# One-token transformer block with cached attention: the values of six of eight steps loaded and multiplied four heads at a time

## The chip, the cores and the metric

The kernel runs on one core of a Trainium2 chip, in fp32 throughout. Five engines work side by side, each through its own list of instructions in order: PE (TensorE, matrix products; its weight loads are shown as PEld), DVE (VectorE), ACT (ScalarE), POOL (GpSimd) and SP (SyncE, which here only issues loads and stores). A wait on a semaphore holds up everything behind it on the same engine. Loads are carried by 16 DMA engines. The metric is device time in microseconds (us) of one execution, lower is better.

## What is computed

Batch 2, one new token, model width 512, 32 query heads that share 8 key/value heads (4 to 1), head width 128. Keys and values come from caches of 32768 positions, of which only the last W = 4096 are read. All weights and the cache window, 97.5 MB, are read once.

```python
mod = (silu(c) @ w_mod).reshape(2, 6, 1, 512)        # sa, ca, ga, sb, cb, gb
h = layernorm(x) * (1 + ca) + sa
q = (h @ wq)                                         # 2 x 32 heads x 128
p = softmax(q . k_cache[:, :, -4096:] * 128**-0.5)   # 4 query heads per key head
x = x + ga * ((p . v_cache[:, :, -4096:]) @ wo)
h = layernorm(x) * (1 + cb) + sb
x = x + gb * (silu(h @ w1) @ w2)
```

## The kernel before

**Loads.** All large loads go through one SBUF ring of 8 slots, 16 KB per partition each (`stream`, lines 70 to 75), in the order in which the program asks for them: `w_mod` (3 slots), `wq` (4 slots), then keys and values of the eight attention steps, then `wo`, `w1`, `w2` in pieces. SP issues all of them. A load into a slot waits until whatever read the slot's old contents is done: DVE for keys, PE for values and weights. The small inputs differ: `c` is loaded by four loads that ACT issues (line 109), `x` by one that SP issues between `w_mod` and `wq` (line 113). Both go into the tile `xc`, which DVE clears first (line 102). Every DMA signals one of eight semaphores, taken in turn over all issuing engines; the ninth DMA takes the first one again and is not issued before the earlier load on that semaphore has landed completely.

**Attention.** There are eight steps. Step s covers two key heads of one batch row (`divmod(s, B)`, line 80), with 4096 KB of keys and 4096 KB of values (`load_pair`, 32 KB per partition). `fetch(s + 1)` asks for the keys of step s + 1 and the values of step s. In a step:

- `keys(s, j)`, j = 0 to 3 (line 349): DVE transposes the keys in 32 x 32 blocks, eight instructions; four buffers hold the results.
- `scores(s, j)` (line 362): PE multiplies them with the queries, 16 products of 512 columns. In the trace every fp32 product is two records.
- `maxima` and `exponentials` (lines 372 to 394): the maxima per query head, a small product that turns them, the bias, the exponential on ACT.
- `turn` (lines 406 to 423): DVE transposes the probabilities (xp) and masks them (zp), PE spreads them with four products (pT), and two ACT copies write them into `ptb`, the weights for the values.
- `weighted` (line 436): 16 products of 512 columns against the values, and an ACT copy of the sum (ob, line 446); `collect` (line 454) adds it into `o_all`.

`turn`, `weighted` and `collect` of a step stand one step later on the engines, beside the key work of the next step. `inorder` keeps what it wraps in program order on its engine; the rest is placed by a scheduler. `place(1)` (lines 303 to 317) prepares the queries of the second half of the heads and stands in step 2.

**The tail.** `o_all` is divided by the row sums (on, line 526) and spread (oq, line 533) into `oTn` (line 536). Then `busy(6)` (line 559) issues six products whose result nothing reads; they keep PE running until `wo` is there. Then come the products with `wo` (acc_o, line 573), the second layer norm, `w1` (hid, line 621), silu, `w2` (acc_yw, acc_y, acc_l, lines 655 to 680) and the store (line 698).

Of the kernel before, what the change touches and what calls it, by code (L numbers as in the profile page):

```python
# [23 lines left out]
def adaln_block(  # L24
# [45 lines left out]
    def stream(n=1):  # L70
# [3 lines left out]
        turn_of[0] = i + n  # L74
        return slots[:, i % RING : i % RING + n, :].rearrange("p s e -> p (s e)")

    def load_pair(cache, s):


        i, b = divmod(s, B)  # L80
        t = stream(2)
        nc.sync.dma_start(
            t,
            cache[b, 2 * i : 2 * i + 2, SK - W :, :].rearrange("e (u n) d -> u e (n d)", u=P // 2),
        )
        return t

    def load_runs(w, per, lo, hi):
# [17 lines left out]
    rows8 = lambda t: t.rearrange("(ab r) m -> ab r m", r=16)[:, 0, :]  # L106
    for b in range(B):
        for lo in (0, 2):
            nc.scalar.dma_start(
                c_sp.rearrange("(g y) m -> g y m", g=4)[lo : lo + 2, 16 * b, :],  # L110
                c[b].rearrange("(g m) -> g m", m=P)[lo : lo + 2],
            )
    nc.sync.dma_start(rows8(x_sp), x2.rearrange("b (g m) -> g b m", m=P))
    wqt = load_runs(wq, 4, 0, 4)


# [31 lines left out]
        id16[:, :, None].to_broadcast([P, 16, 2]),  # L148
        half[:, None, :].to_broadcast([P, 16, 2]),
    )  # L150
    odd = const([P, 2], "odd")
    nc.vector.tensor_reduce(
        odd, ident.rearrange("p (a r) -> p r a", r=2), axis=AX.X, op=ALU.add
# [15 lines left out]
    nc.gpsimd.tensor_copy(  # L169
        selh[:, :, 2 * HQ - 8 : 2 * HQ].rearrange("p m (e g) -> p m e g", e=2),  # L170
        id4.rearrange("p (e m g) -> p m e g", e=2, g=G),
    )

    quad = const([P, 4, P], "quad")
# [20 lines left out]
    for t in mrow:  # L195
        nc.gpsimd.memset(t, 0.0)

    ptb = [const([P, 16, 2, 16], f"ptb{i}") for i in range(2)]
# [6 lines left out]
    oTn = const([P, 32, 32], "oTn")  # L205
    nc.gpsimd.memset(oTn, 0.0)
    mod_sp = const([P, 4, P], "mod_sp")
    x1 = const([P, P], "x1")

# [124 lines left out]
    kt, vt, wot, kT = {}, {}, [], {}  # L334
    s_ps, pr, o_ps, o_sb = {}, {}, {}, {}

    def fetch(s):

        if s < STEPS:
            kt[s] = load_pair(k_cache, s)  # L340
        if s > 0:
            vt[s - 1] = load_pair(v_cache, s - 1)

    def keys(s, j):


        kT[s, j] = ktp.tile([P, 64, 32], F32, tag="kT", name=f"kT{s}_{j}")
        for c in range(2):
            inorder(nc.vector.transpose(  # L349
                kT[s, j][:, 32 * c : 32 * c + 32, :],  # L350
                kt[s].rearrange("p (n j r) -> p j n r", j=4, r=32)[:, j, 32 * c : 32 * c + 32, :],
            ))

    def scores(s, j):

        if j == 0:
            s_ps[s] = bank("A", f"s{s}")
        i, b = divmod(s, B)
        for c in range(2):
            for e in range(2):  # L360
                r, h = 64 * e + 32 * c, 2 * i + e
                inorder(nc.tensor.matmul(  # L362
                    s_ps[s][r : r + 32, :],
                    qbd[h // 4][:, h % 4, b, j, :],
                    kT[s, j][:, 32 * c : 32 * c + 32, e:32:2],
                    start=(j == 0),
                    stop=(j == 3),
                ))
# [17 lines left out]
        ))  # L386

    def exponentials(s):
        bp = bank("B", f"bp{s}")
# [4 lines left out]
        inorder(nc.scalar.activation(  # L394
            pr[s].rearrange("p t k -> p (t k)"),
            s_ps[s],
            AF.Exp,
            bias=bias,
            scale=SCALE,
            accum_out=rowsum[:, s : s + 1],  # L400
        ))

    def turn(s):

        xp = once.tile([P, 16, 32], F32, tag="xp", name=f"xp{s}")
        inorder(nc.vector.transpose(xp, pr[s]))  # L406
        zp = once.tile([P, 4, 16, 16], F32, tag="zp", name=f"zp{s}")
        inorder(nc.vector.tensor_mul(  # L408
            zp,
            xp[:, None, :, 0:16].to_broadcast([P, 4, 16, 16]),  # L410
            quarter[:, :, None, None].to_broadcast([P, 4, 16, 16]),
        ))
        tp = bank("C", f"pT{s}")[:, : 2 * P]
        for i in range(4):
            inorder(nc.tensor.matmul(  # L415
                tp[32 * i : 32 * i + 32, :],
                mix.rearrange("p v e -> p (v e)"),
                zp.rearrange("p y t x -> p (y t) x")[:, :, 4 * i : 4 * i + 4],
                start=True,
                stop=True,  # L420
            ))
        for e in range(2):
            inorder(nc.scalar.activation(  # L423
                ptb[s % 2][:, :, e, :],
                tp.rearrange("p (w z) -> p w z", z=16),
                AF.Copy,
                scale=odd[:, e : e + 1],
            ))

    def weighted(s):  # L430
# [14 lines left out]
        o_sb[s] = once.tile([P, 4 * DH], F32, tag="wide", name=f"ob{s}")  # L445
        inorder(nc.scalar.copy(o_sb[s], o_ps[s]))  # L446

    def collect(s):

        i, b = divmod(s, B)  # L450
        lo = 2 * HQ - 8 - (HQ * b + 2 * G * i)
        for m in range(4):
            r = 64 * (m % 2)
            inorder(nc.tensor.matmul(  # L454
                o_all[r : r + 64, :],
                selh[:, m, lo : lo + 2 * HQ],
                o_sb[s][:, m * DH : (m + 1) * DH],
                start=(s == 0 and m < 2),
                stop=(s == STEPS - 1 and m >= 2),
                skip_group_check=True,  # L460
            ))

    fetch(0)
    keys(0, 0)
    for s in range(STEPS + 1):
        if s < STEPS:
            fetch(s + 1)
            scores(s, 0)
        if s > 0 and s != STEPS - 1:
            turn(s - 1)  # L470
        if s > 1:
            collect(s - 2)
        if s == 2:
            place(1)
        if s < STEPS:
            for j in range(1, 4):
                keys(s, j)
                scores(s, j)
            maxima(s)
            exponentials(s)  # L480
        if s < STEPS - 2:
            keys(s + 1, 0)
        if s > 0:
            weighted(s - 1)
        if s == STEPS - 2:
            turn(s)
            keys(s + 1, 0)
    collect(STEPS - 1)
# [67 lines left out]
    def busy(n):  # L556

        for _ in range(n):
            inorder(nc.tensor.matmul(  # L559
                junk[0:32, :],  # L560
                id4,
                quad.rearrange("p m y -> p (m y)"),
                start=True,
                stop=True,
            ))
# [1 line left out]

    acc = bank("D", "acc_o")
    ao = bank("A", "ao")[:, :P]
    busy(6)  # L570
    for q in range(28):
        g = q % 4
        inorder(nc.tensor.matmul(  # L573
# [152 lines left out]
```

## Time and profile before

| what | value |
|---|---|
| three runs | 235.96, 235.50, 235.21 us; median 235.5 |
| span of the profiled execution (first to last instruction) | 233.6 us |
| what the median has beyond that span | 1.9 us |
| busy PE / PEld / DVE / ACT / POOL | 160.1 / 42.0 / 114.8 / 28.9 / 10.5 us |
| loads and stores on SP's queue | 3768 packets, 97.53 MB, busy 97.2% of 16 engines' span |
| mean granted TensorE clock | 0.927 |

The span lacks what lies around the instructions; the profiled execution's own time is taken as its span plus the 1.9 us by which the median of the runs exceeds it. Rows of the timeline give start and length in us, the engine, the line of the kernel, the operation, out<-in and how many instructions were merged; the bracket behind a row says how long the engine had been idle before and what released it. In the chain of waits each piece starts where the one before released it.

### The profile page before, as it was taken

Reading aid. Unit: us, or ns where it says so; the run is one execution under the profiler, and the core shown is the slowest. Engines: PE = TensorE matmul, PEld = TensorE weight load, DVE = VectorE, ACT = ScalarE, POOL = GpSimd, SP = SyncE. Lnnn points to the kernel's source line nnn. Section 1 sums busy time; section 2 is a strip of 40 time slices with the busy share of each in tenths; the row PEclk is TensorE's granted clock in tenths of the full one; section 3 lists DMA queues with packets and bytes.
Section 4 is the critical chain, followed back from the end, with each engine's and each line's share of the span. In section 5 each row is a group of like instructions: output and inputs, shape, how many; then the busy total and the mean of one; then the engine's idle time right before and its main releaser. Section 6 shows DMA issues by size and latency. Waiting matters only on the chain.

```text
span 233.6 us, 2565 instructions
## 1 busy us (share of the span) xinstructions
PE 160.1 (69%) x1070; PEld 42.0 (18%) x1070; DVE 114.8 (49%) x171; ACT 28.9 (12%) x65; POOL 10.5 (5%) x35
## 2 busy tenths in 40 slices
PE   0004806949687839787679759759769778789784
PEld 0001301201111111211111201201111122324222
DVE  3004310278794758696197179249559540101232
ACT  1100300000311120120210201111030030102020
POOL 8600000000000000000000000000000000000000
PEclk9999965988799976999999979997999997999999
DMA  7998998999999999999999999999999999989991
GB/s 269 438 551 359 393 505 359 440 449 415 415 432 449 436 438 415 421 438 446 443 426 415 424 443 449 438 421 421 424 450 438 443 407 463 463 351 439 425 409 66
DMA packets 3794, 97.68 MB, mean 418 GB/s; under 512 B 432, under 2 KB 456, under 8 KB 968
## 3 DMA queue, kind: packets, MB, share of 16 engines
q1 hardware_dynamic: 3768, 97.53, 97.2%
q8 instruction: 8, 0.13, 0.2%
q14 instruction: 2, 0.02, 0.0%
q10 hardware_dynamic: 16, 0.00, 0.0%
HBM read 97.53 MB, written 0.00 MB: 418 GB/s over the span
## 4 chain that ended last, share of the span: by engine, by line
DMA 60%; issue 18%; DVE 14%; PE 6%; POOL 1%; SPq 0%; POOLq 0%; ACT 0%; DVEq 0%
DMA slots<-in_A_k_cache_dram 22%; DMA slots<-in_A_wq_dram 14%; DMA slots<-in_A_v_cache_dram 12%; DMA slots<-in_B_w_dram 12%; DVE kT L349 11%; PE o L436 2%; PE q L290 2%; DVE zp L408 1%; PE acc_yw L655 1%; DVE xp L406 1%; PE acc_y L665 0%; DVE xc L102 0%; DVE qT L303 0%; POOL qg L307 0%; PE acc_y L546 0%
## 5 line engine op out<-in xcount | busy, mean ns | idle before, releaser
L349 DVE STREAM_TRANSPOSE kT<-slots 128x1024 f32<-128x1024 f32 x64 | 73.7, 1210 | 23.6 <-DMA slots<-in_A_k_cache_dram 23.6
L362 PE MATMUL s<-kT,qbd 128*32 128x512 f32 x256 | 70.5, 703 | 18.9 <-DVE kT L349 17.9
L436 PE MATMUL o<-slots,ptb 128*32 128x512 f32 x256 | 30.8, 624 | 2.1 <-DMA slots<-in_A_v_cache_dram 2.1
L362 PEld LDWEIGHTS s<-kT,qbd 128*32 128x32 f32 x256 | 9.9, 114 | 69.5 <-DVE kT L349 65.1
L259 PE MATMUL m_a<-slots,scT 128*32 128x256 f32 x32 | 2.9, 446 | 20.5 <-DVE scT L251 20.5
L290 PE MATMUL q<-slots,hq_T 128*32 128x512 f32 x64 | 8.7, 707 | 9.0 <-DMA slots<-in_A_wq_dram 9.0
L436 PEld LDWEIGHTS o<-slots,ptb 128*32 128x32 f32 x256 | 8.1, 113 | 17.9 <-issue 17.8
L392 ACT COPY bias<-bp 128x1 f32<-128x1 f32 x8 | 1.3, 159 | 77.1 <-PE bp L390 77.1
L372 DVE TENSOR_REDUCE mx<-s 128x1 f32<-128x512 f32 x8 | 5.5, 692 | 9.5 <-PE s L362 9.5
L559 PE MATMUL junk<-quad,id 128*32 128x512 f32 x22 | 10.2, 595 | 0.0
L408 DVE TENSOR_TENSOR zp<-xp,quarter 128x1024 f32<-128x1024 f32 x8 | 9.8, 1225 | 0.2
L423 ACT ACTIVATE ptb<-pT,odd 128x256 f32<-128x256 f32 x16 | 6.7, 473 | 25.7 <-PE pT L415 25.7
L303 DVE STREAM_TRANSPOSE qT<-q 128x512 f32<-128x512 f32 x2 | 1.4, 718 | 14.2 <-PE q L290 12.7
L446 ACT COPY ob<-o 128x512 f32<-128x512 f32 x8 | 4.7, 586 | 25.9 <-PE o L436 25.9
L415 PE MATMUL pT<-zp,mix 128*32 128x256 f32 x64 | 5.5, 416 | 3.0 <-DVE zp L408 2.9
L374 PE MATMUL mT<-ident,mx 128*1 128x128 f32 x16 | 3.0, 271 | 6.3 <-DVE mx L372 6.3
L406 DVE STREAM_TRANSPOSE xp<-pr 128x512 f32<-128x512 f32 x8 | 5.5, 685 | 3.6 <-ACT pr L394 3.6
L245 DVE STREAM_TRANSPOSE cT<-xc 128x128 f32<-128x128 f32 x1 | 0.4, 403 | 13.9 <-DMA xc<-in_c_dram 13.9
L573 PE MATMUL acc_o<-slots,oTn 128*32 128x512 f32 x56 | 6.2, 593 | 0.9 <-DMA slots<-in_A_wo_dram 0.9
L544 DVE COPY acc_o_sb<-acc_o 128x256 f32<-128x256 f32 x1 | 0.4, 424 | 12.7 <-ACT acc_o_sb L543 12.7
L390 PE MATMUL bp<-negscale,mrow 1*128 1x1 f32 x16 | 3.0, 254 | 4.3 <-DVE mrow L383 4.3
L454 PE MATMUL o_all<-ob,selh 128*64 128x128 f32 x64 | 5.3, 285 | 0.8 <-ACT ob L446 0.8
(136 smaller groups left out, 92.7 us busy)
## 6 DMA issues: line engine op xcount, KB each, us to landing
slots<-in_A_k_cache_dram SPq DMA_DIRECT2D x8, 4096.0 KB, 27.7
slots<-in_A_v_cache_dram SPq DMA_DIRECT2D x8, 4096.0 KB, 27.7
slots<-in_w_mod_dram SPq DMA_DIRECT2D x1, 6144.0 KB, 17.1
slots<-in_A_wo_dram SPq DMA_DIRECT2D x1, 6144.0 KB
slots<-in_B_w_dram SPq DMA_DIRECT2D x1, 2688.0 KB
slots<-in_A_wo_dram SPq DMA_DIRECT2D x1, 2048.0 KB, 29.5
slots<-in_B_w_dram SPq DMA_DIRECT2D x1, 2048.0 KB
slots<-in_B_w_dram SPq DMA_DIRECT2D x1, 896.0 KB
```

Of the source, the lines that this page charges most:

```text
L290: nc.tensor.matmul(q_ps[n][32 * g : 32 * g + 32, :], hq_T[:, k, :], wv[:, n, g], start=(k == 0), stop=(k == 3),)
L349: inorder(nc.vector.transpose(kT[s, j][:, 32 * c : 32 * c + 32, :], kt[s].rearrange("p (n j r) -> p j n r", j=4, r=32)[:, j, 32 * c : 32 * ...
L362: inorder(nc.tensor.matmul(s_ps[s][r : r + 32, :], qbd[h // 4][:, h % 4, b, j, :], kT[s, j][:, 32 * c : 32 * c + 32, e:32:2], start=(j == ...
L372: inorder(nc.vector.tensor_reduce(mx, s_ps[s], axis=AX.X, op=ALU.max))
L406: inorder(nc.vector.transpose(xp, pr[s]))
L408: inorder(nc.vector.tensor_mul(zp, xp[:, None, :, 0:16].to_broadcast([P, 4, 16, 16]), quarter[:, :, None, None].to_broadcast([P, 4, 16, 16 ...
L415: inorder(nc.tensor.matmul(tp[32 * i : 32 * i + 32, :], mix.rearrange("p v e -> p (v e)"), zp.rearrange("p y t x -> p (y t) x")[:, :, 4 * ...
L423: inorder(nc.scalar.activation(ptb[s % 2][:, :, e, :], tp.rearrange("p (w z) -> p w z", z=16), AF.Copy, scale=odd[:, e : e + 1],))
L436: inorder(nc.tensor.matmul(o_ps[s][r : r + 32, :], ptb[s % 2][:, w].rearrange("p e z -> p (e z)"), vt[s].rearrange("p (c w m f d) -> p c f ...
L454: inorder(nc.tensor.matmul(o_all[r : r + 64, :], selh[:, m, lo : lo + 2 * HQ], o_sb[s][:, m * DH : (m + 1) * DH], start=(s == 0 and m < 2) ...
L559: inorder(nc.tensor.matmul(junk[0:32, :], id4, quad.rearrange("p m y -> p (m y)"), start=True, stop=True,))
L573: inorder(nc.tensor.matmul(acc[32 * g : 32 * g + 32, :], oTn[:, q, :], wot[q], start=(q < 4), stop=(q >= 24),))
```

## The change

- Steps are counted another way (`spot`): steps 0 and 1 are heads 0 to 3 of batch row 0, steps 2 and 3 the same heads of row 1, steps 4 to 7 heads 4 to 7.
- The values of steps 0 to 5 come in three loads of four heads each (`load_four`: 8192 KB, 64 KB per partition, four ring slots), asked for behind the keys of the two steps that they belong to. The values of steps 6 and 7 come as pairs, behind the keys of step 7.
- `turn` of steps 0 to 5 makes eight spreading products rather than four, and two ACT copies of 512 columns rather than 256 into `ptq`, a tile that also holds `ptb` and `oTn`. `weighted_four` makes 64 products of 256 columns for each load (the same number of columns as two `weighted`), one copy and two `collect` products.
- `turn` of an odd step now stands ahead of the keys of the next step. `weighted(6)` and `weighted(7)` stand after the last `turn`.
- All large and small loads of lines 82 to 113 are issued by SP, `c` by four loads and `x` by four rather than one; the loads of keys and values are kept in program order.
- `busy(6)` becomes `busy(9)`.

```diff
+    def spot(s):
+        return s // (2 * B) * 2 + s % 2, s // 2 % B
...
+    def load_four(cache, p):
+        t = stream(4)
+        inorder(nc.sync.dma_start(
+            t,
+            cache[p % B, p // B * 4 : p // B * 4 + 4, SK - W :, :].rearrange(
+                "e (u n) d -> u e (n d)", u=P // 4
+            ),
+        ))
+        return t
...
     for b in range(B):
         for lo in (0, 2):
-            nc.scalar.dma_start(
+            nc.sync.dma_start(
                 c_sp.rearrange("(g y) m -> g y m", g=4)[lo : lo + 2, 16 * b, :],
...
-    nc.sync.dma_start(rows8(x_sp), x2.rearrange("b (g m) -> g b m", m=P))
+    for b in range(B):
+        for lo in (0, 2):
+            nc.sync.dma_start(
+                x_sp.rearrange("(g y) m -> g y m", g=4)[lo : lo + 2, 16 * b, :],
+                x2[b].rearrange("(g m) -> g m", m=P)[lo : lo + 2],
+            )
...
         if s < STEPS:
             kt[s] = load_pair(k_cache, s)
-        if s > 0:
-            vt[s - 1] = load_pair(v_cache, s - 1)
+        if s % 2 and s // 2 < BIG:
+            vb[s // 2] = load_four(v_cache, s // 2)
+        if s == STEPS - 1:
+            for t in range(2 * BIG, STEPS):
+                vt[t] = load_pair(v_cache, t)
...
+        for w in range(64):
+            r = 32 * (w % 4)
+            inorder(nc.tensor.matmul(
+                o_ps[p][r : r + 32, :],
+                ptq[:, w].rearrange("p h z -> p (h z)"),
+                v[:, w // 32, w // 16 % 2, w // 8 % 2, w % 8],
...
-    for s in range(STEPS + 1):
-        if s < STEPS:
+    for s in range(STEPS):
+        if s % 2 == 0 and s > 0:
+            weighted_four(s // 2 - 1)
+        if s + 1 < STEPS:
             fetch(s + 1)
-            scores(s, 0)
-        if s > 0 and s != STEPS - 1:
+        scores(s, 0)
+        if s % 2:
             turn(s - 1)
...
+        if s % 2:
+            turn(s)
+        if s + 1 < STEPS:
+            keys(s + 1, 0)
+    nc.gpsimd.memset(oTn, 0.0)
+    for s in range(2 * BIG, STEPS):
+        weighted(s)
+        collect(s)
...
-    busy(6)
+    busy(9)
```

Three places of the instruction order matter below. First SP at the start of the program. The brackets are the waits ahead of an instruction: DMAHW0 to DMAHW7 are the eight semaphores of the loads, the engine names those of the engines. Before:

```order
L93 DMA slots<-in_w_mod_dram 128x12288
L113 DMA xc<-in_A_x_dram 8x1x128 [waits DVE_49]
L93 DMA slots<-in_A_wq_dram 128x16384
L82 DMA slots<-in_A_k_cache_dram 128x1x8192 [waits DMAHW0_49,PE_49]
L82 DMA slots<-in_A_k_cache_dram 128x1x8192 [waits PE_49]
```

The same place after the change:

```order
L108 DMA slots<-in_w_mod_dram 128x12288
L124 DMA xc<-in_c_dram 2x128 [waits DVE_49]
L124 DMA xc<-in_c_dram 2x128 x3
L130 DMA xc<-in_A_x_dram 2x128 x3
L130 DMA xc<-in_A_x_dram 2x128 [waits DMAHW0_49]
L108 DMA slots<-in_A_wq_dram 128x16384 [waits DMAHW1_49]
L86 DMA slots<-in_A_k_cache_dram 128x1x8192 [waits DMAHW2_49,PE_49]
```

The load of `w_mod` has semaphore 0, the eight small loads have 1 to 7 and 0 again. So the last load of `x` stands behind the landing of `w_mod`, and `wq` behind it on SP; before, nothing but the clearing of `xc` stood between `w_mod` and `wq`.

The second place is the last loads of keys and values on SP. Before (steps 5 to 7; keys and values alternate):

```order
L82 DMA slots<-in_A_k_cache_dram 128x1x8192
L82 DMA slots<-in_A_v_cache_dram 128x1x8192
L82 DMA slots<-in_A_k_cache_dram 128x1x8192
L82 DMA slots<-in_A_v_cache_dram 128x1x8192
L82 DMA slots<-in_A_k_cache_dram 128x1x8192
L82 DMA slots<-in_A_v_cache_dram 128x1x8192 x2
```

After (steps 4 to 7):

```order
L86 DMA slots<-in_A_k_cache_dram 128x1x8192 x2
L95 DMA slots<-in_A_v_cache_dram 128x1x16384
L86 DMA slots<-in_A_k_cache_dram 128x1x8192 x2
L86 DMA slots<-in_A_v_cache_dram 128x1x8192 x2
L108 DMA slots<-in_A_wo_dram 128x12288
```

Counted in places of 4096 KB from the first keys on, the keys of step 6 moved from place 12 to place 13; the keys of step 7 stand directly behind them at place 14, as before, and the values of steps 6 and 7 at places 15 and 16, as before.

The third place is PE between the last scores and the products with `wo`; bp is the last product of the exponentials of step 7, pT and o those of `turn` and `weighted`. Before:

```order
L390 MATMUL bp_850<-negscale,mrow_142 128x1
L436 MATMUL o_856<-slots,ptb_145 32x512 x16
L415 MATMUL pT_879<-zp_877,mix 32x256 x4
L514 MATMUL lp<-ones,rx 64x1 x2
L454 MATMUL o_all<-ob_873,selh 64x128 x4
L436 MATMUL o_890<-slots,ptb_146 32x512 x16
L454 MATMUL o_all<-ob_907,selh 64x128 x4
L533 MATMUL oq<-on,quad 128x64 x4
L559 MATMUL junk<-quad,id_58 32x512 x6
L573 MATMUL acc_o<-slots,oTn 32x512 x28
```

After:

```order
L442 MATMUL bp_951<-negscale,mrow_156 128x1
L611 MATMUL lp<-ones,rx 64x1 x2
L487 MATMUL pT_961<-zp_959,mix 32x256 x4
L508 MATMUL o_969<-slots,ptq 32x512 x16
L552 MATMUL o_all<-ob_986,selh 64x128 x4
L508 MATMUL o_992<-slots,ptq 32x512 x16
L552 MATMUL o_all<-ob_1009,selh 64x128 x4
L630 MATMUL oq<-on,quad 128x64 x4
L656 MATMUL junk<-quad,id_58 32x512 x9
L670 MATMUL acc_o<-slots,ptq 32x512 x28
```

The value products of step 6 moved from ahead of the last pT to behind it, and nine products that nothing reads stand ahead of acc_o where there were six.

More of the change, by code (lines that the diff above doesn't have):

```diff
@@ L196, in adaln_block @@
         nc.gpsimd.memset(t, 0.0)
-    ptb = [const([P, 16, 2, 16], f"ptb{i}") for i in range(2)]
+    ptq = const([P, 64, 4, 8], "ptq")
+    ptb = [
+        ptq[:, 16 * i : 16 * i + 16].rearrange("p w h z -> p (w h z)").rearrange(
+            "p (w e z) -> p w e z", w=16, e=2
+        )
+        for i in range(2)
+    ]
     qbd = [const([P, 4, B, 4, 32], f"qbd{n}") for n in range(2)]
@@ L203, in adaln_block @@
     rowsum = const([P, HKV], "rowsum")
-    oTn = const([P, 32, 32], "oTn")
-    nc.gpsimd.memset(oTn, 0.0)
+    oTn = ptq[:, 32:64].rearrange("p w h z -> p w (h z)")
     mod_sp = const([P, 4, P], "mod_sp")
@@ L457, in collect @@
                 o_sb[s][:, m * DH : (m + 1) * DH],
-                start=(s == 0 and m < 2),
+                start=False,
                 stop=(s == STEPS - 1 and m >= 2),
```

92 lines of the change are left out of this document (71 added, 21 removed).

## The prediction

> **What bounds the kernel now.** I read the page first, then the chain of waits, then the timeline of the start and of the tail.
>
> ```profile
> DMA  7998998999999999999999999999999999989991
> q1 hardware_dynamic: 3768, 97.53, 97.2%
> 36.80:193.20 156.40, 120.11 (x704) 27.22 (x704) 100.54 (x117) 20.44 (x52) 0.98 (x4) 0.92 1.00 432
> ```
>
> The first two rows are the page's DMA slices and its load queue; the third, from the table by stretch, is the attention part (length, then busy PE, PEld, DVE, ACT, POOL, clock, DMA share, GB/s). The DMA engines are busy 97.2% of the span, and in the attention all the time (share 1.00), while PE and DVE have 36 and 56 us to spare. The idle DMA time lies at the two ends.
>
> ```profile
> 127.07 27.67 DMA slots<-in_A_k_cache_dram
> 165.80 27.66 DMA slots<-in_A_v_cache_dram
> 193.46 0.14 issue
> 193.60 5.37 PE o L436 x32
> 198.99 27.29 DMA slots<-in_B_w_dram
> 226.28 0.14 issue
> 226.42 1.92 PE acc_yw L655 x16
> ```
>
> The chain of waits says the same: a load lands, a little work frees a slot, the next load of the chain takes 27 us in a full queue. The keys of step 6 land at 154.74 (127.07 + 27.67), the values of step 7 at 193.46. These are places 12 and 16, so a 4096 KB place takes 38.72 / 4 = 9.68 us. After the last values PE has work, but acc_yw again waits for a load. So a change can do two things here: stop the load stream for a while, which shifts everything behind it, or make the compute between the last keys and acc_yw later than the loads.
>
> **The start: the stream stops once.** This is the first term.
>
> ```profile
> 0.73 0.38 SPq L93 DMA_DIRECT2D slots<-in_w_mod_dram  x1
> 3.32 0.61 SPq L93 DMA_DIRECT2D slots<-in_A_wq_dram  x1
> 2.58 2.62 ACTq L109 DMA_DIRECT2D xc<-in_c_dram  x4
> slots<-in_w_mod_dram SPq DMA_DIRECT2D x1, 6144.0 KB, 17.1
> slots<-in_A_wq_dram SPq DMA_DIRECT2D x1, 33.8
> ```
>
> These are issues of the timeline and the page's times from issue to landing. `w_mod` lands at 0.73 + 17.1 = 17.83; `wq` had been queued behind it since 3.32 and lands at 37.12 without a gap. After the change the last load of `x` is the ninth DMA and takes semaphore 0, so SP waits until 17.83 before it issues it. A small load costs its issuer 2.62 / 4 = 0.66, so `wq` is issued at 18.5, when the queue has run dry. Into a dry queue, `w_mod` needed 17.1 for 6144 KB, of which 1.5 places x 9.68 = 14.5 are transfer and 2.6 are start and landing. So `wq` (8192 KB, 19.4) lands at 18.5 + 2.6 + 19.4 = 40.4, which is 3.3 later. Nothing can hide this, since no load is left idle later to make it good. Bounds: at least the 0.7 of the issue, if the start overlaps it wholly; at most 4.
>
> The smaller edits of the start are worth nothing: `c` and `x` land right behind `w_mod`, which the products there need anyway. DVE reaches the moments of `x` at 20.4, and the last part of `x` should land about 2 after its issue at 17.83.
>
> **The larger loads.** `wq` already has 64 KB per partition: it took 37.12 - 17.83 = 19.29 for two places, against 19.36 for keys and values. Three such loads save 0.2. By that the stream behind `wq` is 3.1 later than before.
>
> **The middle: does a load come late?** A load of four heads waits for all 64 products on the one before it.
>
> ```profile
> 83.09 0.72 DVE L303 STREAM_TRANSPOSE qT<-q 128x512 f32<-128x512 f32 x1 [1.49 <-PE o_all L454]
> 85.91 6.88 DVE L349 STREAM_TRANSPOSE kT<-slots 128x1024 f32<-128x1024 f32 x6
> 65.26 0.64 PE L415 MATMUL pT<-zp,mix 128*32 128x256 f32 x8 [0.62 <-DVE zp L408]
> 65.96 0.84 ACT L423 ACTIVATE ptb<-pT,odd 128x256 f32<-128x256 f32 x2 [2.85 <-PE pT L415]
> 214.16 1.08 PE L582 MATMUL ao<-slots,oTn 128*32 128x128 f32 x32
> ```
>
> The tightest is the third such load (values of steps 4 and 5), which waits for the products of steps 2 and 3. Place 5, the keys of step 2, lands at 193.46 - 11 x 9.68 + 3.1 = 90.1. From there to pT of the second step it is 30.2 minus the 0.6 of pT (worked out below) plus 2.8 for `place(1)`; pT with twice the records takes 1.1, and two ACT copies of twice the columns about 1.3: 124.8. The 64 products have the columns of two `weighted`, and 32 short records at 1.08 show that four run at once and that weight loads don't hold them up. So they take 2 x 3.64 to 3.64 + 5.34 (rows below): done at 132 to 134. The place ahead of this load, 10, lands at 138.5; the first DMA engines run dry some 1.5 before, and a load needs 1.5 from issue to first data, so 135.5 is the limit. It holds, with 1.5 to 3.5 to spare. The second load's chain lacks `place(1)` and has that much more room; the pairs at the end wait for nothing later.
>
> **The tail: steps 6 and 7 in a row.** Before, the keys of step 7 came two places after those of step 6, and step 6 was done by then. Now they come one place after, and DVE gets both steps at once.
>
> ```profile
> 174.16 9.13 DVE L349 STREAM_TRANSPOSE kT<-slots 128x1024 f32<-128x1024 f32 x8 [1.95 <-DMA slots<-in_A_k_cache_dram]
> 184.48 0.69 DVE L372 TENSOR_REDUCE mx<-s 128x1 f32<-128x512 f32 x1 [1.19 <-PE s L362]
> 185.89 0.18 DVE L383 COPY mrow<-mg 1x64 f32<-1x64 f32 x1
> 189.90 0.61 PE L415 MATMUL pT<-zp,mix 128*32 128x256 f32 x8
> 154.76 2.37 DVE kT L349 x2
> 157.13 0.60 DVE xp L406
> 158.99 6.80 DVE kT L349 x6
> ```
>
> The first four rows are step 7 of before, the other three (the chain) are keys of step 6 with a `turn` between them, which is what step 7 now looks like. Keys of step 6: 9.13, then 1.19 until the maxima start, then 185.89 + 0.18 - 184.48 = 1.59 until DVE is free for the next keys. Step 7: 165.79 - 154.76 = 11.03 with the `turn` of step 6 inside, 1.2 to the maxima, then 189.90 + 0.61 - 184.48 = 6.03 to the end of pT. The sum is 30.2. The keys of step 6 are now at place 13: 154.74 + 9.68 + 3.1 = 167.5. PE therefore begins the values of step 6 at 197.7, although both value loads have landed (193.46 + 3.1 = 196.6 for step 7).
>
> ```profile
> 186.44 3.64 PE L436 MATMUL o<-slots,ptb 128*32 128x512 f32 x32
> 193.60 5.34 PE L436 MATMUL o<-slots,ptb 128*32 128x512 f32 x32 [2.13 <-DMA slots<-in_A_v_cache_dram]
> 199.69 0.66 PE L454 MATMUL o_all<-ob,selh 128*64 128x128 f32 x8 [0.75 <-ACT ob L446]
> 200.87 1.10 PE L533 MATMUL oq<-on,quad 128*128 128x64 f32 x8 [0.53 <-DVE on L526]
> 201.91 5.34 PE L559 MATMUL junk<-quad,id 128*32 128x512 f32 x12
> 208.16 6.21 PE L573 MATMUL acc_o<-slots,oTn 128*32 128x512 f32 x56 [0.91 <-DMA slots<-in_A_wo_dram]
> ```
>
> Value products took 3.64 when PE had been at work, and 5.34 after an idle 2.13. In the new tail PE has only small products between the scores of step 7 and pT, with a pause of some 2, so I take 5.34 for step 6 and 3.64 for step 7. With the copy and `collect`, step 6 takes 200.35 - 193.60 = 6.75, and step 7 5.05; from there to the end of oq are 201.97 - 200.35 = 1.62. That is 211.1. Now nine products nobody reads: 18 records in place of 12, which start every (5.34 - 0.59) / 11 = 0.43, so 7.7: acc_o begins at 218.9. `wo` lands 3.1 later than its 208.1, at 211.2. So the products that once filled a wait are now on the path.
>
> About this row the Trainium skill, "TensorE: Matmul & The Clock Gate", section "Part 1: The HAM clock gate", says that PE falls to half rate after an idle window of about 3.4 us. By that rule a pause of 2 would leave PE at full rate and the sum would be 1.7 lower; the trace shows the half rate after 2.13, and I go by the trace.
>
> ```profile
> 217.67 0.17 DVE L612 TENSOR_TENSOR hT_b<-dT,cbT 128x8 f32<-128x8 f32 x1
> 219.45 1.71 PE L621 MATMUL hid<-slots,hT_b 128*32 128x448 f32 x16 [1.04 <-DMA slots<-in_B_w_dram]
> 221.40 1.71 PE L621 MATMUL hid<-slots,hT_b 128*32 128x448 f32 x16
> 225.34 0.21 DVE L651 TENSOR_TENSOR uT<-z,sgh 128x28 f32<-128x28 f32 x1
> ```
>
> Behind acc_o, before, hid and acc_yw waited for loads; now these are there. From acc_o to hT_b it is 217.84 - 208.16 = 9.7, hid without its wait 3.7, from there to uT 225.55 - 223.11 = 2.4: acc_yw at 218.9 + 15.8 = 234.7. Its load, 226.28 + 3.1, is 5 earlier. From acc_yw to the end it stays 233.6 - 226.4 = 7.2, so the span is 241.9. With the 1.9 between span and median that is **243.8 us**. In terms: 3.1 from the gap, 6.1 from the later value products (211.1 against 201.97, less the gap), 2.6 from junk, less 3.5 of waits for loads that were there before.
>
> **The rivals.**
>
> *PE stays at full rate* in the step 6 products: 243.8 - 1.7 = 242.1. The small products between may keep it so; the row of 5.34 speaks against it. This is the case that the section of the Trainium skill named above gives.
>
> *The loads still set the end.* If DVE catches up or the tail's work is shorter than its rows, only the gap is left: 235.5 + 3.1 = 238.6. For it speaks that acc_yw waits for a load before; against it that 5 us would have to go.
>
> *A load of four heads comes late.* If the products before it take 3 longer than the slack, the queue runs dry and all behind it moves: 246 to 247. The share of 1.00 shows no such gap before, but then a pair was released by half as many products.
>
> *Faster.* The larger pieces may move at another rate, at the place of the three value loads. The page's second slice row speaks for it, with 551 GB/s in a slice in which the 64 KB pieces of `wq` begin.
>
> ```profile
> GB/s 269 438 551 359 393 505 359 440 449 415 415 432 449 436 438 415 421 438 446 443 426 415 424 443 449 438 421 421 424 450 438 443 407 463 463 351 439 425 409 66
> ```
>
> At that rate six places take 58.1 x 432 / 551 = 45.5 and the time would be 231.2; it becomes faster than before from some 504 GB/s on. The 19.29 that `wq` took as a whole speaks against it: a slice books a piece where it begins.
>
> *Heads far apart.* Four heads lie one cache row of 32768 positions apart. If that halved the rate of the three loads, they would cost 58 more, about 300. Keys already come from two such heads at the full 9.68. The Trainium skill, "DMA: Bandwidth & Descriptors", section "Latency and other measured facts", gives such a halving for row pitches of large powers of two; no row here shows it.
>
> That the change doesn't do what it says can be left out: the loads stand in the order as described.
>
> **How the numbers follow.** Chances: forecast 0.42, full rate 0.24, loads set the end 0.12, late load 0.11, faster rate 0.03, heads apart 0.01; and 0.07 that neither gap nor tail comes as worked out, which lies around the old time, up to 1.5 to either side. Measurement tells 0.3% (0.7 us) from no change. So slower 0.42 + 0.24 + 0.12 + 0.11 + 0.01 and 0.01 of the rest, 0.91; no change 0.03; faster 0.06. The range takes in the loads-set-the-end case less half a microsecond for a shorter gap (238.1), and at the top the forecast with a gap of 4 and some of a late load (245.6).
>
> **What would show it.** In the changed profile: a dip in the DMA slices near 18 us and `wq` landing near 40; SP waiting for `w_mod` ahead of a small load; share 1.00 in the attention; the values of step 6 starting some 30 after the keys of step 6, junk ending after `wo` has landed, and acc_o and acc_yw released by PE or DVE, not by a load. It is wrong if `wq` lands at 37, or if acc_yw waits for its load.

## The result, and the profile after

The changed kernel takes 244.73 us (median of 4 runs, 244.44 to 246.08), the kernel before 235.47 on the same chip: 1.0403 times as long, 95% interval 1.0374 to 1.0432. The profiled execution of the changed kernel took 245.0 with a span of 243.0; so 2.0 lie around the span (before 1.9).

The page of the changed kernel: the DMA slices and the queues.

```profile
DMA  7969989999989999989899999899999999999920
q1 hardware_dynamic: 3356, 97.53, 93.8%
q8 instruction: 10, 0.16, 0.2%
```

The third slice (12 to 18 us) shows a dip that was not there before, and the idle end of the row has grown from one slice to two. The bytes are the same; only the share fell, from 97.2% to 93.8%.

The chain of waits of the changed kernel, its first pieces and one further on:

```profile
0.73 17.16 DMA slots<-in_w_mod_dram
17.91 0.47 SPq L130
18.42 21.82 DMA slots<-in_A_wq_dram
...
60.71 29.48 DMA slots<-in_A_k_cache_dram
```

Before, the load of `wq` waited in the queue from 3.32. Now SP stands at line 130 (a load of `x`) until `w_mod` has landed at 17.89; `wq` is issued at 18.42 and lands at 40.24, 3.1 after its 37.12 of before. The keys of step 2 land at 90.19. In the table of waits SP's own row names what held it:

```profile
SPq L130 <- DMA slots<-in_w_mod_dram: 11.4, 1, 11.4
```

The timeline of the changed kernel, middle and tail (in places with rows of other engines between them):

```profile
124.29 8.84 PE L526 MATMUL oq<-slots,ptq 128*32 128x256 f32 x128 [1.38 <-ACT ptq L478]
133.20 0.54 SPq L95 DMA_DIRECT2D slots<-in_A_v_cache_dram  x1
...
167.72 9.13 DVE L400 STREAM_TRANSPOSE kT<-slots 128x1024 f32<-128x1024 f32 x8 [9.77 <-DMA slots<-in_A_k_cache_dram]
...
196.02 0.34 PE L611 MATMUL lp<-ones,rx 128*64 128x1 f32 x4 [2.19 <-DVE rx L600]
197.17 1.08 PE L487 MATMUL pT<-zp,mix 128*32 128x256 f32 x8 [0.82 <-DVE rl L619]
198.00 6.08 PE L508 MATMUL o<-slots,ptq 128*32 128x512 f32 x32
205.39 3.64 PE L508 MATMUL o<-slots,ptq 128*32 128x512 f32 x32
210.98 1.10 PE L630 MATMUL oq<-on,quad 128*128 128x64 f32 x8 [0.53 <-DVE on L623]
212.01 7.48 PE L656 MATMUL junk<-quad,id 128*32 128x512 f32 x17
219.36 6.14 PE L670 MATMUL acc_o<-slots,ptq 128*32 128x512 f32 x52
229.41 2.01 PE L718 MATMUL hid<-slots,hT_b 128*32 128x448 f32 x16
235.87 1.92 PE L752 MATMUL acc_yw<-slots,uT 128*32 128x512 f32 x16
```

The third four-head load is issued at 133.20, in time. From the keys of step 6 (167.72) on, no product waits for a load any more: junk, acc_o, hid and acc_yw, which before had loads in their brackets or right behind them, now follow one another. In the chain of waits, too, no load stands behind the keys of step 2 (90.19). PE works on the values of steps 4 and 5 until 170.5 and has caught up with the scores of step 6 just as DVE ends their keys (176.85). The 9.3 us thus look like a gap of some 3 at the start and a tail that PE and DVE set; the experiments take the two apart.

### The profile page after: what moved, and what is told of

Same layout as the page of the kernel before. It is cut to its first block, busy times and chain, and to the rows that moved or that the text cites. A ratio compares the mean times of both kernels' runs of the same rounds, so it can differ in the third digit from the quotient of the medians.

```text
span 243.0 us, 2986 instructions
## 1 busy us (share of the span) xinstructions
PE 167.6 (69%) x1280; PEld 51.9 (21%) x1280; DVE 114.9 (47%) x172; ACT 29.2 (12%) x62; POOL 11.8 (5%) x42
## 3 DMA queue, kind: packets, MB, share of 16 engines
q1 hardware_dynamic: 3356, 97.53, 93.8%
## 4 chain that ended last, share of the span: by engine, by line
PE 47%; DMA 28%; DVE 18%; ACT 3%; issue 2%; POOL 0%; SPq 0%; DVEq 0%; ACTq 0%
PE s L413 15%; DMA slots<-in_A_k_cache_dram 12%; DVE kT L400 10%; DMA slots<-in_A_wq_dram 9%; PE oq L526 7%; DMA slots<-in_w_mod_dram 7%; PE junk L656 5%; PE q L335 4%; PE o L508 4%; PE pT L469 3%; PE acc_o L670 2%; DVE zp L460 2%; DVE mx L423 2%; PE hid L718 1%; DVE xp L458 1%
## 5 line engine op out<-in xcount | busy, mean ns | idle before, releaser
L413 PE MATMUL s<-kT,qbd 128*32 128x512 f32 x256 | 61.4, 674 | 6.8 <-DVE kT L400 5.9
L526 PE MATMUL oq<-slots,ptq 128*32 128x256 f32 x384 | 27.7, 459 | 4.1 <-ACT ptq L478 4.1
L526 PEld LDWEIGHTS oq<-slots,ptq 128*32 128x32 f32 x384 | 13.5, 131 | 19.5 <-issue 7.0
L469 PE MATMUL pT<-zp,mixq 128*32 128x256 f32 x96 | 9.9, 549 | 11.0 <-DVE zp L460 10.9
L335 PE MATMUL q<-slots,hq_T 128*32 128x512 f32 x64 | 9.8, 780 | 9.5 <-DMA slots<-in_A_wq_dram 9.5
L656 PE MATMUL junk<-quad,id 128*32 128x512 f32 x28 | 12.7, 595 | 0.0
L478 ACT ACTIVATE ptq<-pT,fourth 128x512 f32<-128x512 f32 x12 | 7.6, 683 | 24.5 <-PE pT L469 24.5
L508 PE MATMUL o<-slots,ptq 128*32 128x512 f32 x64 | 9.7, 760 | 0.0
L469 PEld LDWEIGHTS pT<-zp,mixq 128*32 128x32 f32 x96 | 3.8, 141 | 17.3 <-issue 17.0
L670 PE MATMUL acc_o<-slots,ptq 128*32 128x512 f32 x56 | 7.0, 593 | 0.0
```

The source lines that it names most:

```text
L335: nc.tensor.matmul(q_ps[n][32 * g : 32 * g + 32, :], hq_T[:, k, :], wv[:, n, g], start=(k == 0), stop=(k == 3),)
L413: inorder(nc.tensor.matmul(s_ps[s][r : r + 32, :], qbd[h // 4][:, h % 4, b, j, :], kT[s, j][:, 32 * c : 32 * c + 32, e:32:2], start=(j == ...
L469: inorder(nc.tensor.matmul(tq[32 * i : 32 * i + 32, 2 * P * q : 2 * P * q + 2 * P], mixq[:, s % 2, q].rearrange("p u b e -> p (u b e)"), z ...
L478: inorder(nc.scalar.activation(ptq[:, :, h, :], tq.rearrange("p (w z) -> p w z", z=8), AF.Copy, scale=fourth[:, h : h + 1],))
L508: inorder(nc.tensor.matmul(o_ps[s][r : r + 32, :], ptb[s % 2][:, w].rearrange("p e z -> p (e z)"), vt[s].rearrange("p (c w m f d) -> p c f ...
L526: inorder(nc.tensor.matmul(o_ps[p][r : r + 32, :], ptq[:, w].rearrange("p h z -> p (h z)"), v[:, w // 32, w // 16 % 2, w // 8 % 2, w % 8], ...
```

## The experiments

Each result is the median, and the ratio to the kernel before on the same chip, which took 235.47 to 235.59 each time.

**The start alone.** The kernel before, with `c` issued by SP and `x` in four loads:

```
-            nc.scalar.dma_start(
+            nc.sync.dma_start(
...
-    nc.sync.dma_start(rows8(x_sp), x2.rearrange("b (g m) -> g b m", m=P))
+    for b in range(B):
+        for lo in (0, 2):
+            nc.sync.dma_start(
```

> The kernel before with only the start of the change: c in four and x in four loads, all issued by SP. Theory (the stream stops once and the loads set the end): wq lands near 40.3, and 235.5 + 3.1 = 238.6 us (238.0 to 239.2). Rival (a stop at the start is made good later): 235.5.

239.38 us, 1.0161 [1.0147, 1.0176]: 3.8 more. Its chain of waits:

```profile
18.39 21.96 DMA slots<-in_A_wq_dram
...
169.00 27.66 DMA slots<-in_A_v_cache_dram
200.49 28.97 DMA slots<-in_B_w_dram
```

The landings are 40.35, 196.66 and 229.46, which is 3.2 later each than 37.12, 193.46 and 226.28: the gap goes through to the end in full. The time is 0.2 above the range that I expected: of its 3.8, the landings account for 3.2, and no run shows where the other 0.6 lies.

**The start without the ninth load.** The reverse: the changed kernel with `x` in one load.

```
-    for b in range(B):
-        for lo in (0, 2):
-            nc.sync.dma_start(
...
+    nc.sync.dma_start(rows8(x_sp), x2.rearrange("b (g m) -> g b m", m=P))
```

> The changed kernel with x loaded by one load as before; c stays with SP in four. Seven DMAs up to wq, so no semaphore comes round again ahead of it. Theory (wq waits for w_mod only because the ninth DMA takes the first semaphore again): wq is issued near 7 us and lands near 37.1, the DMA slices have no dip near 18 us, and all behind is 3.1 earlier: 244.7 - 3.1 = 241.6 us (241.2 to 242.1). Rival (it is c behind w_mod on SP's queue that stops the stream): wq still lands near 40 and 244.7 stays. Rival (the tail of compute doesn't hang on the loads): wq at 37.1, but 244.7 stays.

241.99 us (240.85 to 243.65), 1.0279 [1.0223, 1.0336], 2.7 less than the changed kernel. The chain of waits shows `wq` landing at 37.27 again:

```profile
5.60 31.67 DMA slots<-in_A_wq_dram
```

**The queue alone.** That leaves open whether it is the ninth DMA or SP's longer list of small loads. The kernel before with `c` issued by SP, `x` still one load:

```
-            nc.scalar.dma_start(
+            nc.sync.dma_start(
```

> The kernel before with c issued by SP in four loads and x in one, so that seven DMAs stand up to wq and no semaphore comes round. Theory (only the semaphore makes the stop, not the queue): wq is issued near 7 and lands near 37.1, 235.5 us (235.2 to 235.9). Rival (small loads on SP's queue between the two large ones stop the stream): 237 or more.

235.63 us, 1.0009 [0.9997, 1.0021]. SP reaches `wq` in its timeline at 5.45, long before `w_mod` lands, and nothing is lost:

```profile
5.45 0.44 SPq L93 DMA_DIRECT2D slots<-in_A_wq_dram  x1
```

So five small loads on SP cost nothing. The stop comes only when the ninth DMA takes the first semaphore again, and SP's row in the table of waits above names the landing of `w_mod` as what it waits for.

**Nine junk products where loads set the pace.** The kernel before with `busy(9)` in place of `busy(6)`:

> The kernel before with nine products that nothing reads instead of six. Theory (they cost only where PE is late): before, junk ended 1.1 ahead of wo, and hid and acc_yw waited 2.5 more for loads, so 2.6 more of junk makes acc_o begin 1.5 later and the end stays: 235.5 us (235.2 to 235.9). Rival (each such product costs its time wherever it stands): 238.1.

235.49 us, 0.9996 [0.9987, 1.0005]. The timeline of this kernel:

```profile
193.65 3.64 PE L436 MATMUL o<-slots,ptb 128*32 128x512 f32 x32 [2.11 <-DMA slots<-in_A_v_cache_dram]
...
200.26 7.91 PE L559 MATMUL junk<-quad,id 128*32 128x512 f32 x18
208.14 6.21 PE L573 MATMUL acc_o<-slots,oTn 128*32 128x512 f32 x56
```

The junk fills waits for loads, and the end stays. I had expected acc_o 1.5 later, yet it begins at 208.14 (before 208.16): in this execution the value products of step 7 took 3.64 after a pause of 2.11, not 5.34 as in the profile before after one of 2.13. The time left over took in the added junk. So the pause alone doesn't make these products slow; the part on the clock comes back to it.

**Fewer junk products where PE sets the pace.** The changed kernel with `busy(6)`, and with none:

> The changed kernel with six products that nothing reads instead of nine, that is with this one edit undone. Theory (the three more were on the path in full): 6 records at 0.43 less, 244.7 - 2.6 = 242.1 us (241.4 to 242.7). Rival (they keep PE at full rate for what follows, and without them the same time is lost in acc_o): 244 or more.

> The changed kernel without the nine products that nothing reads. Theory (they stand on the path, since wo has landed when they begin): acc_o begins at 212.1 instead of 218.9; acc_yw would be ready near 228 and then waits for the first piece of w2, which landed at 229.7, so 236.9 for the span and 238.6 us in runs (238 to 239.2). Rival (PE falls to half rate without them and acc_o takes 3 us longer): the same end or up to 240.5, with acc_o's first products at half rate. Rival (the loads set the end already): 244.7 stays.

242.48 us, 1.0289 [1.0261, 1.0317], and 240.51 us, 1.0209 [1.0184, 1.0233]: 2.3 and 4.2 less than the changed kernel. Three junk products (six records, 2.6 at 0.43 each) cost on this path about what they take. Leaving out all nine (7.35 us of PE up to acc_o) gains only 4.2, as the timeline of the kernel without them shows:

```profile
212.05 7.89 PE L670 MATMUL acc_o<-slots,ptq 128*32 128x512 f32 x56 [0.42 <-DVE ptq L633]
...
230.41 1.92 PE L752 MATMUL acc_yw<-slots,uT 128*32 128x512 f32 x16 [0.47 <-DMA slots<-in_B_w_dram]
```

acc_o takes 7.89 where it took 6.14 to 6.21 behind the junk (the granted clock was 0.50 from 212.06 to 215.48), and then acc_yw waits for its load: the floor of the late loads is reached. The time is where the rival of half rate put it (up to 240.5), above the 239.2 of the theory.

**The value products of step 6 earlier.** The changed kernel with `weighted(6)` ahead of the last `turn`:

```
+        if s == STEPS - 1:
+            weighted(s - 1)
...
-    for s in range(2 * BIG, STEPS):
-        weighted(s)
-        collect(s)
+    collect(STEPS - 2)
+    weighted(STEPS - 1)
+    collect(STEPS - 1)
```

> The changed kernel with the value products of step 6 put on PE right behind the exponentials of step 7, ahead of the last turn, as they stood before the change; its collect behind the turn. Theory (they wait for pT though their values and weights are there): they begin near 193.9, run at full rate in 3.6, and step 7's begin near 199 instead of 205.4, so oq ends near 205.7, junk near 213.3, and acc_yw waits for its load at 229.7 again: 238.7 us (238 to 239.5). Rival (DVE's two steps in a row set it, the order on PE doesn't matter): 243 to 244.7.

240.23 us (239.71 to 241.64), 1.0208 [1.0167, 1.0248], 4.5 less. The timeline and, last, its chain of waits:

```profile
194.07 3.64 PE L508 MATMUL o<-slots,ptq 128*32 128x512 f32 x32
197.53 0.61 PE L487 MATMUL pT<-zp,mix 128*32 128x256 f32 x8
204.77 1.10 PE L632 MATMUL oq<-on,quad 128*128 128x64 f32 x8 [0.53 <-DVE on L625]
231.21 1.92 PE L754 MATMUL acc_yw<-slots,uT 128*32 128x512 f32 x16 [0.77 <-DMA slots<-in_B_w_dram]
```

```profile
202.89 28.19 DMA slots<-in_B_w_dram
```

oq is 6.2 earlier than in the changed kernel, the products and pT run at full rate, and the end is again set by a load. That load lands at 231.08, though: 1.7 later than the gap alone gives (226.28 + 3.1), which puts the time 0.7 above the range that I expected.

**PE kept at work through the pause.** The changed kernel with three products nobody reads (six records) ahead of lp, where PE paused 2.19:

```
+        if s == STEPS - 1:
+            fill(3, "warm")
```

> The changed kernel with three products that nothing reads in PE's pause behind the last exponentials (193.8 to 196.0), none of them on the path. Theory (the pause makes PE fall to half rate, which made pT 1.08 instead of 0.64 and step 6's products 6.1 instead of 3.6): pT 0.64, step 6 3.6, the end 2.5 to 2.9 earlier: 242.0 us. Rival (by the Trainium skill, TensorE: Matmul & The Clock Gate, a pause of 2.2 is shorter than the idle window of about 3.4 and PE was at full rate; something else made these products slow): 244.7.

242.48 us (242.13 to 244.93), 1.0317 [1.0266, 1.0368]: 2.3 less, although work was added. In the timeline:

```profile
194.79 2.76 PE L564 MATMUL warm<-quad,id 128*32 128x512 f32 x6
198.13 0.64 PE L487 MATMUL pT<-zp,mix 128*32 128x256 f32 x8 [0.36 <-DVE zp L460]
198.58 3.62 PE L508 MATMUL o<-slots,ptq 128*32 128x512 f32 x32
...
210.15 9.12 PE L665 MATMUL junk<-quad,id 128*32 128x512 f32 x17
```

pT and the products are back at 0.64 and 3.62. The profiled execution was the slowest of its runs (244.93): here the junk had a stretch of half clock (0.50 from 210.07 to 213.49) and took 9.12 rather than 7.48. That the filling helps at its place is shown by these rows beside those of the five traces with the same tail and the pause left open (the changed kernel, `x` in one load, six and no junk products, and the late kernel that follows), where pT took 1.08 each time and the products 4.62 to 6.11. What it gains in the end hangs on where the next half-clock stretch falls.

**How far the third load is from late.** The changed kernel with five products nobody reads ahead of the value products of steps 2 and 3:

```
+            if s == 4:
+                fill(5, "late")
```

> The changed kernel with five products that nothing reads ahead of the 64 products on the values of steps 2 and 3. PE is thereby 4.3 us later (at half rate up to 4.3 instead of 2.2) there, and so is the issue of the next load of four heads, which was at 133.2. Theory (that load had only about 1.5 to 2 us to spare before the queue ran dry): issue near 136.5 to 137.5, a dip in the DMA share there, and all behind it 1.5 to 2.5 later: 246.2 to 247.2 us. Rival (much more to spare): the load still in time, 244.7. Rival (it was at its limit already): 248.5 or more.

246.13 us (245.35 to 247.63), 1.0446 [1.041, 1.0483], 1.4 more. The timeline:

```profile
128.54 7.07 PE L526 MATMUL oq<-slots,ptq 128*32 128x256 f32 x122
135.69 0.54 SPq L95 DMA_DIRECT2D slots<-in_A_v_cache_dram  x1
...
199.60 6.11 PE L508 MATMUL o<-slots,ptq 128*32 128x512 f32 x32
```

The load is issued 2.49 later (135.69 against 133.20), 0.8 less late than the range that I expected, and the time is just below its range. The dip is there: by the packets in the trace the DMA engines stood idle from 136.24 on, 0.41 us on average of the 16; in the changed kernel they never did in the attention. The kernel with `weighted(6)` early happened to issue this load at 134.38, and there it was 0.05. So the changed kernel had some 1.2 to spare at this place, and it was not used up. The keys of step 6 land 1.6 later (169.31 against 167.69), and the tail starts 1.6 later (199.60 against 198.00).

**What remains.** The changed kernel with `x` in one load and `weighted(6)` early (the two edits above together), once with `busy(9)` and once with `busy(4)`:

> The changed kernel with x in one load and with step 6's value products ahead of the last turn. Theory (gap and tail are the whole of the loss, the large loads themselves cost and bring almost nothing): no gap, acc_yw waits for its load as in the kernel before, 235.3 us (235.0 to 236.0), the same as before or 0.2 less. Rival (the large loads are slower or let the queue run dry): 237 or more. Rival (large loads are faster, and the gap and the tail hid it): 234.5 or less.

> The changed kernel with x in one load, with step 6's value products ahead of the last turn, and with four products that nothing reads instead of nine. Without the last of the three, 1.9 us were left against the kernel before, and its trace had junk from 204.1 to 213.3 while wo had landed at 208. Theory (what was left is junk on the path, half of it at half rate): acc_o begins near 208.2 to 209, acc_yw waits for its load near 226.4, and the time is that of the kernel before within 0.3: 235.3 to 236.0 us. Rival (the loads of four heads themselves cost the 1.9, by pieces that take longer or by more loading of instructions on one DMA engine): 237 or more, with acc_yw waiting for a load that lands later than 227.

237.44 us (236.38 to 239.17), 1.0085 [1.0053, 1.0118], and 237.94 (237.02 to 239.0), 1.01 [1.0081, 1.012]. The gains add up (2.7 + 4.5 = 7.2, measured 7.3), but both kernels stay some 2 above the kernel before, where I had expected at most 0.5 for either. In the timeline of the first (its slowest execution, 239.17), PE is again late, by two half-clock stretches:

```profile
190.71 5.34 PE L503 MATMUL o<-slots,ptq 128*32 128x512 f32 x32
204.14 9.18 PE L653 MATMUL junk<-quad,id 128*32 128x512 f32 x17
...
229.70 1.92 PE L749 MATMUL acc_yw<-slots,uT 128*32 128x512 f32 x16
```

In the second the junk is out of the way, and loads set the end; a row of its timeline and one of its chain of waits:

```profile
210.46 7.91 PE L667 MATMUL acc_o<-slots,ptq 128*32 128x512 f32 x56 [3.78 <-DMA slots<-in_A_wo_dram]
```

```profile
200.14 28.36 DMA slots<-in_B_w_dram
```

`wo` is there at 210.46 (before 208.16) and the `w2` piece at 228.50 (before 226.28): both 2.2 to 2.3 late, without a gap at the start. So neither the gap nor the tail is what is left in this execution, but landings.

The trace also keeps 16 landing signals for each load, as many as there are DMA engines. They name no engine, but show how far apart its parts land. Before, the 16 of the `wo` load that acc_o waits for came between 206.06 and 208.02. Here 15 of them came between 206.43 and 208.12, and the last alone at 210.32. Of the `w2` piece, 14 came by 226.27 (before, all by 226.28), and the other two at 227.45 and 228.49. So the delay of the landing lies in one or two of its 16 parts, not in all of them.

**More TensorE instructions alone.** The changed kernel issues more instructions (2986 against 2565 in all, 10 loads of 16 KB of instructions against 8). The kernel before with 264 tiny products nobody reads, in PE's waits for turned keys:

```
+        if s < 6:
+            tiny(44, f"tiny{s}")
```

> The kernel before with 264 tiny products more (32 columns each, 44 in each of the first six steps, their result read by nobody), placed where TensorE waits about 2.9 us for turned keys. They cost 528 more TensorE instructions, about what the changed kernel has more than the kernel before, and little TensorE time on no path. Theory A, the remaining 2 us of the changed kernel without its gap and its late tail come from the two more loads of 16 KB of instructions, which lie on single DMA engines and make the slowest engine late: the instruction queue shows 10 loads instead of 8, the products acc_o begin at 209 to 210.5 (before 208.2), released by the load of wo, and the time is 236.5 to 237.8. Rival B, the four-head loads themselves make one engine late: 8 or 10 instruction loads, acc_o at 208.2, and the time stays within 0.3 of 235.5.

236.65 us (236.52 to 237.01), 1.0045 [1.003, 1.006], 1.06 more. The queue row of its page, and its chain of waits:

```profile
q8 instruction: 12, 0.20, 0.3%
```

```profile
127.01 27.69 DMA slots<-in_A_k_cache_dram
...
165.76 29.07 DMA slots<-in_A_v_cache_dram
198.67 28.84 DMA slots<-in_B_w_dram
```

The loads and their order are those of before, and still the values of step 7 land at 194.83 and `w2` at 227.51, 1.4 and 1.2 later; the time lies where theory A had it, and rival B's 235.5 is outside. There are 12 instruction loads, though, not the 10 that I expected (each product is two records, as every fp32 product here), and the keys of step 6 land at 154.70 as before, after eight such loads against four. So how many there are doesn't alone set the delay.

The landing signals tell the rest. Behind the first instruction load (at 41.3, one packet of 16 KB that took 0.9), 15 signals of the next large load lie within 0.5, and the last is 1.3 behind them. More instruction loads bring more late signals, but up to the eighth the last signal is never more than 2.1 behind the first; the keys of step 6 spread from 152.98 to 154.70. The ninth instruction load is at 158.91, and in the next large load 15 signals come by 164.37 and the last at 165.65. From then on the last one is 2.9 to 3.1 behind the first. In the kernel before, with eight such loads, it is never more than 2.2. The step is as large as the first one, as if the same engine had been hit a second time.

## Why the prediction was right, point by point

**The gap.** Right in cause and size: predicted 3.3 at `wq` and 3.1 behind it, measured 3.1 at `wq` in the changed kernel and 3.2 at the three landings of the start alone. In the times of the two kernels that undo it or make it alone it is 2.7 and 3.8; what the 3.8 has beyond the landings is open.

**The larger loads** were to save 0.2. They save nothing that shows: from `wq`'s landing to the keys of step 6 there are now 167.72 - 40.24 = 127.5 for 13 places, before 154.74 - 37.12 = 117.6 for 12, which is 9.81 and 9.80 for a place. This also settles two rivals: heads that lie far apart cost no rate, and the four-head loads have no faster one.

**The middle.** Right: the products were to be done at 132 to 134, the load was issued at 133.20. The limit of 135.5 was about 1 too late: issued at 134.38 the load already left a trace of idle DMA time (0.05), at 135.69 it left 0.41.

**The tail.** The order of the work was right. Two terms were too small. The value products of step 6 began 0.3 late and took 6.08, not 5.34, since the half clock covered nearly all of them (196.10 to 202.93); with less junk than worked out, most of acc_o was 0.5 late (219.36 against 218.9; three of its records ran at 218.91 beside the last junk). From acc_o to acc_yw it was 16.5, not 15.8, with a first half of hid at 2.01 rather than 1.71. That makes 1.2 at acc_yw (235.87 against 234.7), and is the 1.1 by which the span (243.0 against 241.9) and the 0.9 by which the time exceeded the forecast.

**The clock.** I had weighed the row of 5.34 against the rule of the Trainium skill, "TensorE: Matmul & The Clock Gate", section "Part 1: The HAM clock gate" (half rate only after an idle window of about 3.4 us), and gone by the row. The changed kernel has the half rate after pauses of 2.19 and 0.82 with only small products between, so as a rule on single pauses it doesn't hold here. But my reason, the pause of 2.13, doesn't hold either. The same records after pauses of 2.11 to 2.34 took 3.64 in three of the five traces with the order of before (the start alone, nine junk products, the tiny products) and 5.34 in the other two. In the changed tail they were slow in all five traces that leave the pause open, by 5.4 on average. So the 5.34 had about the right size for this tail, by luck.

The clock records of the 14 traces show what decides. The granted clock is 0.50 or 1.00, and changes only on a grid of 3.41 us: its stretches last 3.41, 6.83, 10.24 and so on. The same section says that the window runs free of the program, and the traces agree: the grid lies elsewhere in each execution. Two stretches of the changed kernel (length, busy PE first, clock third from the end):

```profile
192.69:196.10 3.41, 0.61 (x7) 0.41 (x6) 1.44 (x5) 0.94 (x3) 0.00 (x0) 1.00 1.03 447
196.10:202.93 6.83, 6.01 (x36) 1.98 (x40) 1.23 (x3) 0.84 (x2) 0.00 (x0) 0.50 0.99 426
```

PE was busy 0.61 of the 3.41 ahead of the half clock, so a stretch with little work is enough; it need not be idle. Taken over all grid stretches of the 14 traces at full clock, the 73 with PE busy less than 40% were all followed by half clock and the 470 with more than 63% all by full clock; of the 106 between, 36 were followed by half clock. At half clock the 86 with PE busy less than 80% were followed by half clock again, and 109 of the other 110 by full. This is why the pause gave 5.34 in the profile before (PE busy 1.28 of the 3.41 ahead) and 3.64 with nine junk products, where the grid split the pause over two stretches (2.04 and 2.59).

**The terms don't add as I wrote them.** I had 6.1 for later value products and 2.6 for junk beside a gap of 3.1. Taking away one cause gave 4.5 (order), 4.2 (all junk) and 2.7 (gap), because behind both causes in the tail stands the floor of the loads. The rival "the loads still set the end", 238.6, had this right as a floor, though not as the outcome: with the junk or the late products gone, acc_yw waits for a load again, at 240.2 to 240.5.

**What I had not priced** is in that floor: 240.2 rather than 238.6. It is the about 2 us that remain with gap and tail both mended. More TensorE instructions alone give 1.1 of it; the landings of `wo` and `w2` give 2.2. The landing signals put this on one or two parts of the queue, and in the kernel with the tiny products the step comes with the ninth instruction load. In the second mended kernel one comes at 201.23, ahead of `wo`, and the last signal falls from 0.7 behind the others (values of step 7) to 2.2 (`wo`). So the loads of instructions are the cause as far as these times can show it; that a second one falls on the same DMA engine is read from the size of the step, as no view names the engine, and what picks the engine stays open. In the profiled execution of the first mended kernel the half-clock stretches set the end instead.

## What to carry to other kernels

Count DMAs against the semaphores before splitting a small load: one more load than there are semaphores, placed ahead of a large one, made every later landing 3.1 to 3.2 us late, while five small loads on the same queue cost nothing. In a kernel bound by loads, look at what comes between the last load and the end before regrouping the work: the value products here were as many as before, but two steps' worth came behind the last keys, and products that had filled a wait for free became 4 us of the path. When the bound is the queue, take the instruction count as traffic too, and look at the last landing signal of a load, not only at the queue's mean share.

## What the runs showed of the hardware

264 tiny products in pauses of TensorE, with no change to any data load, made the last loads land 1.2 to 1.4 us later. The Trainium skill, "Runtime: NRT & Kernel Launch", section "Instruction fetch mechanics", tells that code is refilled in blocks of 16 KiB and that the cost is mostly hidden. The blocks are in this profile (12 packets with 0.20 MB); with a full data queue the added products were not hidden, at 1.06 us. The delay is in the last one or two of a load's 16 landing signals.

TensorE's half-clock stretches move. The same 17 records of junk took 7.48 in the changed kernel, 9.12 with the earlier pause filled and 9.18 in the first of the two mended kernels, and the runs of the changed kernel and its variants spread by 1.4 to 2.8 us where those of the kernel before, beside them, spread by 0.3 to 0.9. One stretch of 3.41 us at half clock over full work costs 1.7 us (5.34 against 3.64). So a PE row of one profiled execution behind a stretch with little PE work can be 1.7 us off, and more where a second stretch follows, as in the 6.08.
